# The opening of a fused attention and mixer kernel: batch 1's first transposes one unit earlier, their loads earlier, two dummies, and a new list of PSUM banks

## The chip, the cores and the metric

The kernel runs on one core of one Trainium2 chip. The metric is the device time of one execution in microseconds, and of several executions the median counts. A core has five engines that run side by side and meet at semaphores: TensorE (PE in the profile; its weight loads are PEld), VectorE (DVE), ScalarE (ACT), GpSimd (POOL) and SyncE (SP). TensorE writes to PSUM, which the other engines read and empty. In this kernel POOL's queue issues all loads of q, k, v and of the weights except the very first piece of k, and SP's queue issues the stores and the transposes that are done by DMA.

## The reference

The kernel computes sigmoid attention for 8 batches, 12 heads, 448 positions and a head width of 64, lays the heads side by side as 768 channels, and sends the result through a mixer with a token layer and a channel layer:

```python
S = q.shape[2]
scores = np.matmul(q, k.transpose(0, 1, 3, 2)) / np.sqrt(q.shape[-1]) - np.log(S)
attn = 1.0 / (1.0 + np.exp(-scores))
x = np.matmul(attn, v).transpose(0, 2, 1, 3).reshape(B, S, H * D)

h = np.maximum(x.transpose(0, 2, 1) @ w_tok1, 0.0) @ w_tok2
u = x + h.transpose(0, 2, 1)
out = u + np.maximum(u @ w_ch1, 0.0) @ w_ch2
```

w_tok1 is 448x256, w_tok2 256x448, w_ch1 768x1536 and w_ch2 1536x768. Everything comes in as float32; the loads cast to 16 bits.

## The kernel before

**Units and cycles.** The 12 heads of a batch are worked in three units of four heads, so 8 batches give 24 cycles of one unit each. A unit's 448 positions are seven tiles of 64 (index j). `qk(b, u, j)` makes the scores of one tile: four matmuls of 64x64 into one of two score buffers, and then one sigmoid on ScalarE (line 182) from there into `att`. `av` multiplies `att` by v, tile by tile, into two accumulators (`xa`), and VectorE casts them into `xT` (line 211). `xtrans` turns `xT` into `xn` with 8 transposes on TensorE and one copy on VectorE (lines 235 and 240). `tok1` is the first token layer (8 matmuls, line 280, and a relu), `ytrans` the second (4 matmuls, line 301, and two additions on VectorE, line 308). `ch1` and `ch2` are the channel layers.

**How q and k get their layout.** Scores need q and k with the head width on partitions. For the first units `pe_transpose(b, t, u)` does this on TensorE: 14 transposes of 128x64 (line 155) into one PSUM tile, and one VectorE copy into `tr_q` or `tr_k` (line 164). From batch 2's second unit on it is done by DMA. The transposes of batch 1's unit 0 need only the loads of batch 1's q and k for unit 0, which go into tiles of their own.

**The order of the work is written out by hand.** Each engine takes its instructions in the order in which the program issues them. For batch 0 the list `between` (lines 625 to 653) says what follows each of the seven score tiles of each of the three units; the loop at line 654 issues score tile j and then the entry j. In unit 0 the entries are dummy matmuls (`keep_warm`, line 582, on a tile of zeros into a bank called `heat`, which nobody reads) and transposes for batch 0's later units. In unit 1 they are the values of unit 0, its `xtrans` and its `tok1`, with three empty entries (2, 3 and 5); in unit 2 they are the values of unit 1, the second token layer of unit 0, the transposes of batch 1's unit 0, `xtrans` and `tok1`. Batch 1's unit 0 (lines 662 to 682) is written out too: the rest of batch 0's token layers, the transposes for batch 1's unit 1 and the first pieces of the channel layer. From line 701 on, cycles 4 to 8 take pieces of the channel layers between the scores by shares.

**Loads.** They go out on POOL's queue in the order of lines 500 to 556, each `load` as two DMAs, one for each half of the partitions. At most eight of them are open: where a ninth is due, POOL waits for the oldest.

**Banks.** PSUM has eight banks. The two score buffers take four; everything else takes one of four banks, m0 to m3, through `bank()` (line 79). Up to cycle 8 the digit is read from the string `OPENING_BANKS`, one character for each allocation in the order of issue; after that the banks go round. An accumulator waits until the readers of the one that last stood in its bank are done. So the string decides which earlier readers each accumulator waits for.

Of the kernel before, what the change touches and what calls it, by code (L numbers as in the profile page):

```python
# [20 lines left out]
NJ = 7  # L21
NP = 64
NU = 3
OPENING_BANKS = "0321302130213021213021303021302121302130130210321032103210321021301301201"


@with_exitstack
def kernel(
# [46 lines left out]

    opening_banks = [int(n) for n in OPENING_BANKS]
    at_bank = [0]

    def bank(shape, dtype, name):

        if opening_banks:
            n = opening_banks.pop(0)
        else:
            n = at_bank[0]
            at_bank[0] = (n + 1) % 4
        return pp.tile(shape, dtype, tag=f"m{n}", bufs=1, name=name)
# [7 lines left out]
    def raw_tile(b, t):  # L94
        if (b, t) not in raw:
            tag, bufs = f"raw_{t}", 2 if t == "v" else 1
            if b == 1 and t != "v":
                tag = f"rel_{t}"
            raw[b, t] = pa.tile(
                [128, NU, 2, NJ, E], FP16, tag=tag, bufs=bufs, name=f"raw_{t}_{b}"  # L100
            )
        return raw[b, t]

    def load(b, t, src, u0, u1):

        for g in range(2):
            dst = raw_tile(b, t)[64 * g : 64 * g + 64, u0:u1, :, :, :]
            heads = src[b, 6 * g + 2 * u0 : 6 * g + 2 * u1]
            nc.gpsimd.dma_start(
                out=dst.rearrange("p u hi j e -> p (u hi) (j e)"),  # L110
                in_=heads.rearrange("h (p j) e -> p h (j e)", j=NJ),
            )
# [12 lines left out]
    def tr_tile(b, t):  # L125
        if (b, t) not in tr:
            tr[b, t] = pa.tile(
                [128, NU, NJ, 128], FP16, tag=f"tr_{t}", bufs=2, name=f"tr_{t}_{b}"
            )
        return tr[b, t]  # L130
# [18 lines left out]
    def pe_transpose(b, t, u, j0=0, j1=NJ, on_scalar=False):  # L149
        if j0 == 0:  # L150
            tps[t] = bank([128, NJ, 128], FP16, f"tp_{t}_{b}_{u}")
        ps = tps[t]
        for j in range(j0, j1):
            for hi in range(2):
                nc.tensor.transpose(  # L155
                    out=ps[64 * hi : 64 * hi + 64, j, :],
                    in_=raw[b, t][:, u, hi, j, :],
                    identity=ident[:, :],
                )
        dst, src = tr_tile(b, t)[:, u, j0:j1, :], ps[:, j0:j1, :]  # L160
        if on_scalar:
            nc.scalar.activation(out=dst, in_=src, func=COPYF)
        else:
            nc.vector.tensor_copy(out=dst, in_=src)


    def qk(b, u, j):
        if j == 0:
            att[b, u] = pa.tile(
                [128, 2, NJ, S], FP16, tag="att", bufs=2, name=f"att_{b}_{u}"  # L170
            )
        ps = pp.tile([128, 2, 512], FP32, tag="qk", bufs=2, name=f"qk_{b}_{u}_{j}")
        for g in range(2):
            for hi in range(2):
                nc.tensor.matmul(  # L175
                    out=ps[64 * g : 64 * g + 64, hi, 0:S],
                    lhsT=tr[b, "k"][64 * hi : 64 * hi + 64, u, j, 64 * g : 64 * g + 64],
                    rhs=tr[b, "q"][64 * hi : 64 * hi + 64, u, :, 64 * g : 64 * g + 64],
                    start=True,
                    stop=True,  # L180
                )
        nc.scalar.activation(  # L182
            out=att[b, u][:, :, j, :],
            in_=ps[:, :, 0:S],
            func=SIGMOID,
            bias=bias_t[:, :],
            scale=att_scale,
        )
# [42 lines left out]
    def xtrans(b, u):  # L231
        ps = bank([128, 4, 2, 128], FP16, f"xb_{b}_{u}")
        for g in range(2):
            for t in range(4):
                nc.tensor.transpose(  # L235
                    out=ps[:, t, g, :],
                    in_=xTs[b % 2][:, u, g, 128 * t : 128 * t + 128],
                    identity=ident[:, :],
                )
        nc.vector.tensor_copy(  # L240
            out=xn_tile(b)[:, u, :, :, :].rearrange("s g t d -> s t g d"),
            in_=ps[:, :, :, :],
        )
# [3 lines left out]
    def h1_tile(b, u):  # L247
        if u == 0:
            h1[b] = pa.tile([128, 2, 2, NU, 128], FP16, tag="h1", bufs=2, name=f"h1_{b}")
# [19 lines left out]
    def tok1(b, u, relu_on_vector=False, with_scores=False):  # L269

        if not with_scores:
            h1_tile(b, u)
            one = bank([128, 2, 2, 128], FP32, f"tk_{b}_{u}")
            tks[b] = [one[:, tcb, :, :] for tcb in range(2)]
        ps = tks[b]
        for tcb in range(2):
            cols = slice(128 * tcb, 128 * tcb + 128)
            for t in range(3 if with_scores else 4):
                rows = slice(0, 64 if t == 3 and NU * b + u >= N_FIRST else 128)
                nc.tensor.matmul(  # L280
                    out=ps[tcb],
                    lhsT=w1[rows, t, cols],
                    rhs=xn[b][rows, u, :, t, :],
                    start=(t == 0 and not with_scores),
                    stop=(t == (2 if with_scores else 3)),
                )
        for tcb in range(2):
            dst, src = h1[b][:, tcb, :, u, :], ps[tcb]
            if relu_on_vector:
                nc.vector.tensor_scalar(  # L290
                    out=dst, in0=src, scalar1=0.0, scalar2=None, op0=MAX
                )
            else:
                nc.scalar.activation(out=dst, in_=src, func=RELU)  # L294
# [31 lines left out]
    def ch1(b, cb, d0=0, d1=NDB):  # L326
        if cb == 0 and d0 == 0:
            h2[b] = pa.tile([128, NCB, S], FP16, tag="h2", bufs=1, name=f"h2_{b}")
        if d0 == 0:
            acc[b, cb] = bank([128, 512], FP32, f"c1_{b}_{cb}")  # L330
        ps = acc[b, cb]
        for d in range(d0, d1):
            nc.tensor.matmul(  # L333
                out=ps[:, 0:S],
                lhsT=c1[:, BY_UNIT[d], 128 * cb : 128 * cb + 128],
                rhs=uts[b % 2][:, BY_UNIT[d], 0:S],
                start=(d == 0),
                stop=(d == NDB - 1),
            )
        if d1 == NDB:  # L340
            ch1_out(b, cb, ps)

    def ch1_out(b, cb, ps):
        nc.vector.tensor_scalar(  # L344
            out=h2[b][:, cb, :], in0=ps[:, 0:S], scalar1=0.0, scalar2=None, op0=MAX
        )
# [167 lines left out]
    for par in range(2):  # L514
# [3 lines left out]
            in_=tok_rows[0:6].rearrange("(t par) p c -> par p t c", par=2)[par],  # L518
        )
    nc.gpsimd.dma_start(out=w1[0:64, 3, :], in_=tok_rows[NJ - 1])  # L520
    nc.gpsimd.dma_start(
        out=w2s[:, :, :], in_=moe_w_tok2.rearrange("(tc t) s -> t tc s", tc=2)
    )
    load(0, "v", v, 1, NU)
    load(1, "q", q, 0, 1)
    load(1, "k", k, 0, 1)

    def load_c1(half):
        cols = slice(CC // 2 * half, CC // 2 * half + CC // 2)
        nc.gpsimd.dma_start(  # L530
            out=c1[:, :, cols],
            in_=moe_w_ch1.rearrange("(db d) c -> d db c", db=NDB)[:, :, cols],
        )
# [46 lines left out]
    def keep_warm(n):  # L580
        for _ in range(n):
            nc.tensor.matmul(  # L582
                out=heat[0][:, 0:256],
                lhsT=warm[:, 0:128],
                rhs=warm[:, :],
                start=True,
                stop=True,
            )
# [26 lines left out]
    def tp(b, u, t, j0=0, j1=NJ):  # L615
        return lambda: pe_transpose(b, t, u, j0, j1)

    def value(u, j0, j1):
        return lambda: av(0, u, j0, j1)

    def tok(u):
        return lambda: tok1(0, u, relu_on_vector=True)
# [12 lines left out]
        [  # L635
            [value(0, 0, 3)],
            [value(0, 3, NJ)],
            [],
            [],
            [lambda: xtrans(0, 0), regroup_w2],  # L640
            [],
            [tok(0)],
        ],
        [
            [value(1, 0, 3)],
            [lambda: ytrans(0, 0)],
            [value(1, 3, NJ)],
            [tp(1, 0, "q")],
            [lambda: xtrans(0, 1)],
            [tp(1, 0, "k")],  # L650
            [tok(1)],
        ],
    ]
# [10 lines left out]
    ytrans(0, 1)  # L664
    qk(1, 0, 1)
    av(0, 2, 5, NJ)
    pe_transpose(1, "q", 1)
    qk(1, 0, 2)
    xtrans(0, 2)
    pe_transpose(1, "k", 1)  # L670
    qk(1, 0, 3)
    tok1(0, 2, relu_on_vector=True)
    qk(1, 0, 4)
    for cb in range(2):
        ch1(0, cb, 0, 4)
    ytrans(0, 2)
    qk(1, 0, 5)
    for cb in range(2):
# [205 lines left out]
```

## Time and profile before

| | |
|---|---|
| Executions, us | 364.57, 362.68, 362.68 |
| Median, us | 362.68 |
| The profiled execution, us | 364.3 |
| Its span from first to last instruction, us | 362.5 |
| TensorE busy | 354.4 us, 98% of the span |
| VectorE busy | 185.3 us, 51% |
| ScalarE busy | 169.4 us, 47% |
| POOL busy | 52.9 us, 15% |
| Mean granted TensorE clock | 0.993 of full |

The profile is one execution, taken on the chip. Its page gives the busy time of the engines, the chain of work that ended last, and the costliest groups of instructions. The trace behind it can be asked for rows in order of time. A row of the timeline has the start, the length from the first to the last of its instructions, the engine, the line, the operation, output and input, the number of instructions (x4), and in square brackets how long the engine had stood still before them and what ended that. Rows of one engine can overlap a little, since matmuls are pipelined: the distance from one row's start to the next is the better measure. A row of the view by stretches has the stretch, its length, the busy time of PE, PEld, DVE, ACT and POOL, the granted clock of TensorE, the busy share of the DMA engines, and GB/s. The last number of a row of DMA issues is the time from issue to landing. Times are us from the start of the span.

### The profile page before, as it was taken

The numbers are of one execution on the slowest core, as the hardware profiler recorded it, in microseconds if no ns is written. First come the engines' busy times: TensorE is split into PE (matmuls) and PEld (weight loads), VectorE is DVE, ScalarE is ACT, GpSimd is POOL, SyncE is SP. The second block draws the span as 40 slices with busy tenths as digits, with TensorE's granted clock in tenths as the row PEclk, the third lists the DMA queues.
The fourth block names the chain that finished last, engine by engine and source line by source line (L and its number), as shares of the span: only waits on it lengthen the run. The fifth ranks groups of instructions, "written<-read, shape, count | busy, mean of one in ns | idle before, by whom it ended". The sixth has DMA issues, their size and how long they took to land.

```text
span 362.5 us, 9065 instructions
## 1 busy us (share of the span) xinstructions
PE 354.4 (98%) x4028; PEld 203.4 (56%) x4028; DVE 185.3 (51%) x343; ACT 169.4 (47%) x214; POOL 52.9 (15%) x91
## 2 busy tenths in 40 slices
PE   8899999999999999999999999999999999999995
PEld 5545455555556655666556655666556655555563
DVE  3457557354655555456555555456553345526531
ACT  2987645766338840688018840688018840010000
POOL 8875500110040002100040002100010000000000
PEclk9989999999999999999999999999999999999999
DMA  8999999999899697978979497978964490056014
GB/s 146 173 193 205 204 203 190 143 178 214 160 179 178 82 191 142 199 116 151 219 122 189 100 190 141 195 119 150 212 89 84 92 166 12 0 118 140 14 43 109
DMA packets 103958, 52.09 MB, mean 144 GB/s; under 512 B 76016, under 2 KB 100848, under 8 KB 103920
## 3 DMA queue, kind: packets, MB, share of 16 engines
q1 hardware_dynamic: 78880, 29.70, 44.2%
q0 software_dynamic: 24816, 21.50, 38.4%
q8 instruction: 31, 0.51, 0.5%
q10 hardware_dynamic: 224, 0.33, 0.3%
q14 instruction: 7, 0.06, 0.0%
HBM read 43.45 MB, written 11.01 MB: 150 GB/s over the span
## 4 chain that ended last, share of the span: by engine, by line
PE 94%; ACT 4%; DVE 1%; issue 0%
PE c L333 30%; PE c L356 11%; PE c L375 10%; PE qk L175 9%; PE xa L202 8%; PE tk L280 6%; PE c L434 5%; PE yt L301 5%; PE c L458 5%; ACT att L182 4%; PE heat L582 2%; PE tp_k L155 1%; PE tk L261 1%; PE tp_q L155 1%; DVE ut L308 0%; PE xb L235 0%
## 5 line engine op out<-in xcount | busy, mean ns | idle before, releaser
L182 ACT ACTIVATE att<-qk,att_bias 128x896 f16<-128x896 f32 x168 | 155.3, 1017 | 119.3 <-PE qk L175 119.2
L333 PE MATMUL c<-ut,c 128*128 128x448 f16 x576 | 112.7, 353 | 0.0
L333 PEld LDWEIGHTS <-c 128*128 128x128 f16 x576 | 54.7, 98 | 55.7 <-issue 4.9
L344 DVE TENSOR_SCALAR h<-c 128x448 f16<-128x448 f32 x96 | 59.7, 624 | 45.9 <-PE c L333 45.3
L175 PE MATMUL qk<-tr_q,tr_k 64*64 64x448 f16 x672 | 57.2, 358 | 2.1 <-ACT att L182 2.0
L398 DVE TENSOR_TENSOR o<-un,c 128x384 f32<-128x384 f16 x42 | 23.3, 554 | 49.7 <-PE c L434 30.1
L211 DVE CAST xT<-xa 128x448 f16<-128x448 f32 x48 | 27.7, 618 | 37.4 <-PE xa L202 37.4
L356 PE MATMUL c<-c,h 64*64 64x384 f16 x960 | 46.6, 323 | 0.0
L202 PE MATMUL xa<-att,raw_v 64*64 64x448 f16 x672 | 39.9, 353 | 0.7 <-DVE ut L308 0.7
L375 PE MATMUL c<-c,h 128*128 128x384 f16 x216 | 37.8, 326 | 0.0
L356 PEld LDWEIGHTS <-h 64*64 64x64 f16 x960 | 28.1, 107 | 11.8
L175 PEld LDWEIGHTS <-tr_k 64*64 64x64 f16 x672 | 20.3, 105 | 22.2 <-issue 15.6
L308 DVE TENSOR_TENSOR ut<-xT,yt 128x448 f16<-128x448 f16 x48 | 27.4, 613 | 4.8 <-PE yt L301 4.8
L686 POOL COPY gate<-tr_q 128x2 f16<-128x2 f16 x6 | 1.1, 183 | 193.2 <-DMA tr_q<-rel_q 193.2
L294 ACT ACTIVATE h<-tk 128x256 f16<-128x256 f32 x42 | 14.4, 416 | 31.6 <-PE tk L280 31.6
L375 PEld LDWEIGHTS <-h 128*128 128x128 f16 x216 | 20.4, 98 | 14.5 <-issue 1.8
L202 PEld LDWEIGHTS <-raw_v 64*64 64x64 f16 x672 | 20.4, 108 | 12.2 <-issue 1.9
L280 PE MATMUL tk<-xn,w 128*128 128x256 f16 (+1 forms) x156 | 22.6, 282 | 0.0
L301 PE MATMUL yt<-w,h 128*128 128x448 f16 x96 | 22.0, 353 | 0.0
L434 PE MATMUL c<-c,h 128*128 128x384 f16 x120 | 22.0, 326 | 0.0
L280 PEld LDWEIGHTS <-w 128*128 128x128 f16 (+1 forms) x156 | 13.7, 100 | 7.9 <-issue 5.4
L458 PE MATMUL c<-c,h 128*64 128x384 f16 x192 | 17.3, 328 | 0.0
(53 smaller groups left out, 181.0 us busy)
## 6 DMA issues: line engine op xcount, KB each, us to landing
out_dram<-o SPq DMA_DIRECT2D x48, 192.0 KB, 2.8
c<-in_moe_w_ch_dram POOLq DMA_DIRECT2D x4, 1152.0 KB, 15.2
raw_v<-in_v_dram POOLq DMA_DIRECT2D x12, 336.0 KB, 5.9
raw_k<-in_k_dram POOLq DMA_DIRECT2D x10, 336.0 KB, 7.6
raw_q<-in_q_dram POOLq DMA_DIRECT2D x10, 336.0 KB, 10.3
raw_q<-in_q_dram POOLq DMA_DIRECT2D x14, 112.0 KB, 6.1
out_dram<-o SPq DMA_DIRECT2D x15, 96.0 KB, 2.5
raw_k<-in_k_dram POOLq DMA_DIRECT2D x12, 112.0 KB, 5.6
```

Source lines behind the costliest of these rows:

```text
L175: nc.tensor.matmul(out=ps[64 * g : 64 * g + 64, hi, 0:S], lhsT=tr[b, "k"][64 * hi : 64 * hi + 64, u, j, 64 * g : 64 * g + 64], rhs=tr[b, " ...
L182: nc.scalar.activation(out=att[b, u][:, :, j, :], in_=ps[:, :, 0:S], func=SIGMOID, bias=bias_t[:, :], scale=att_scale,)
L202: nc.tensor.matmul(out=ps[g][64 * hi : 64 * hi + 64, 0:S], lhsT=raw[b, "v"][64 * g : 64 * g + 64, u, hi, j, :], rhs=att[b, u][64 * g : 64 ...
L211: nc.vector.tensor_copy(out=xTs[b % 2][:, u, g, 0:S], in_=ps[g][:, 0:S])
L280: nc.tensor.matmul(out=ps[tcb], lhsT=w1[rows, t, cols], rhs=xn[b][rows, u, :, t, :], start=(t == 0 and not with_scores), stop=(t == (2 if ...
L301: nc.tensor.matmul(out=ps[:, 0:S], lhsT=h1[b][:, tcb, g, u, :], rhs=w2[:, tcb, :, :], start=(tcb == 0), stop=(tcb == 1),)
L333: nc.tensor.matmul(out=ps[:, 0:S], lhsT=c1[:, BY_UNIT[d], 128 * cb : 128 * cb + 128], rhs=uts[b % 2][:, BY_UNIT[d], 0:S], start=(d == 0), ...
L344: nc.vector.tensor_scalar(out=h2[b][:, cb, :], in0=ps[:, 0:S], scalar1=0.0, scalar2=None, op0=MAX)
L356: nc.tensor.matmul(out=ps[p][m : m + 64, 0:n], lhsT=lhsT(p, part, m), rhs=rhs(p, part), start=(first and turn == 0), stop=(last and turn = ...
L375: nc.tensor.matmul(out=ps[:, 0:DH], lhsT=h2[b][:, cb, 128 * t : 128 * t + 128], rhs=c2[:, cb, cols], start=(cb == 0), stop=(cb == NCB - 1 ...
L434: nc.tensor.matmul(out=ps[p][:, 0:DH], lhsT=h2[b][:, n, 128 * t : 128 * t + 128], rhs=c2[:, n, DH * p : DH * p + DH], start=False, stop=(n ...
L458: nc.tensor.matmul(out=ps[g], lhsT=h2[b][:, n, 384:448], rhs=c2[:, n, DH * g : DH * g + DH], start=(n == 0), stop=(n == NCB - 1 and not ad ...
```

## The change

The loads of batch 1's unit 0 move forward: q ahead of v's units 1 and 2 and of w_tok2, k ahead of v's unit 2. The load of v's units 1 and 2 becomes two loads. In `between`, unit 1's empty entries 2, 3 and 5 get two dummies, the transposes of q and those of k for batch 1's unit 0. Unit 2's entry 3 becomes empty, and its entry 5 takes the transposes of q for batch 1's unit 1. Behind it, batch 1's unit 0 is left with the transposes of k for unit 1; the first block of the channel layer moves ahead of the token step. `OPENING_BANKS` is a new string with 74 digits where there were 73 (the second `heat` of unit 1 is the additional allocation). What is computed stays the same.

```diff
-OPENING_BANKS = "0321302130213021213021303021302121302130130210321032103210321021301301201"
+OPENING_BANKS = "23103210320103210323210321210321313021302302132013201320132013213023023123"
...
     nc.gpsimd.dma_start(out=w1[0:64, 3, :], in_=tok_rows[NJ - 1])
+    load(1, "q", q, 0, 1)
+    load(0, "v", v, 1, 2)
     nc.gpsimd.dma_start(
         out=w2s[:, :, :], in_=moe_w_tok2.rearrange("(tc t) s -> t tc s", tc=2)
     )
-    load(0, "v", v, 1, NU)
-    load(1, "q", q, 0, 1)
     load(1, "k", k, 0, 1)
+    load(0, "v", v, 2, NU)
...
         [
             [value(0, 0, 3)],
             [value(0, 3, NJ)],
-            [],
-            [],
+            [new_heat, lambda: keep_warm(2)],
+            [tp(1, 0, "q")],
             [lambda: xtrans(0, 0), regroup_w2],
-            [],
+            [tp(1, 0, "k")],
             [tok(0)],
         ],
         [
             [value(1, 0, 3)],
             [lambda: ytrans(0, 0)],
             [value(1, 3, NJ)],
-            [tp(1, 0, "q")],
+            [],
             [lambda: xtrans(0, 1)],
-            [tp(1, 0, "k")],
+            [tp(1, 1, "q")],
             [tok(1)],
         ],
...
     av(0, 2, 5, NJ)
-    pe_transpose(1, "q", 1)
+    pe_transpose(1, "k", 1)
     qk(1, 0, 2)
     xtrans(0, 2)
-    pe_transpose(1, "k", 1)
     qk(1, 0, 3)
+    ch1(0, 0, 0, 4)
     tok1(0, 2, relu_on_vector=True)
     qk(1, 0, 4)
-    for cb in range(2):
-        ch1(0, cb, 0, 4)
+    ch1(0, 1, 0, 4)
     ytrans(0, 2)
```

## The prediction, made before the changed kernel was run

> **What bounds the kernel now.** I read the page's engine shares first, then the clock in short stretches, then TensorE's timeline in the opening, and at last the places behind it where TensorE stands still.
>
> ```profile
> span 362.5 us, 9065 instructions
> PE 354.4 (98%) x4028; PEld 203.4 (56%) x4028; DVE 185.3 (51%) x343; ACT 169.4 (47%) x214; POOL 52.9 (15%) x91
> ```
>
> TensorE is busy for 98% of the span. A microsecond of its work that moves into a hole, or a hole that closes, therefore reaches the end, unless a transfer then comes too late. The holes lie in the opening. The stretches below give the granted clock (the value behind the five engines), and the timeline gives TensorE's steps: each L175 row is one score, and the distance between two of them is what lies between.
>
> ```profile
> 19.80:19.90 0.10, 0.10 (x4) 0.03 (x3) 0.10 (x1) 0.10 (x1) 0.10 (x1) 0.73 1.26 197
> ...
> 23.20:23.30 0.10, 0.10 (x8) 0.08 (x4) 0.00 (x0) 0.10 (x1) 0.10 (x1) 0.71 1.18 215
> ```
>
> ```profile
> 14.33 0.38 PE L175 MATMUL qk<-tr_q,tr_k 64*64 64x448 f16 x4
> ...
> 15.23 0.38 PE L175 MATMUL qk<-tr_q,tr_k 64*64 64x448 f16 x4
> ...
> 17.02 0.38 PE L175 MATMUL qk<-tr_q,tr_k 64*64 64x448 f16 x4 [0.47 <-ACT att L182]
> 17.92 0.38 PE L175 MATMUL qk<-tr_q,tr_k 64*64 64x448 f16 x4 [0.52 <-ACT att L182]
> 18.24 0.62 PE L235 MATMUL xb<-ident,xT 128*128 128x128 f16 x8
> 18.82 0.38 PE L175 MATMUL qk<-tr_q,tr_k 64*64 64x448 f16 x4
> 19.71 0.51 PE L175 MATMUL qk<-tr_q,tr_k 64*64 64x448 f16 x4 [0.52 <-ACT att L182]
> ...
> 21.98 0.59 PE L175 MATMUL qk<-tr_q,tr_k 64*64 64x448 f16 x4
> ...
> 23.37 0.36 PE L175 MATMUL qk<-tr_q,tr_k 64*64 64x448 f16 x4
> ...
> 24.52 0.38 PE L175 MATMUL qk<-tr_q,tr_k 64*64 64x448 f16 x4
> ...
> 25.49 0.36 PE L175 MATMUL qk<-tr_q,tr_k 64*64 64x448 f16 x4
> ...
> 26.29 0.38 PE L175 MATMUL qk<-tr_q,tr_k 64*64 64x448 f16 x4
> ...
> 27.23 0.38 PE L175 MATMUL qk<-tr_q,tr_k 64*64 64x448 f16 x4
> ...
> 28.06 0.38 PE L175 MATMUL qk<-tr_q,tr_k 64*64 64x448 f16 x4
> ...
> 29.35 0.38 PE L175 MATMUL qk<-tr_q,tr_k 64*64 64x448 f16 x4
> ```
>
> In the second unit (14.33 to 19.71) ScalarE's sigmoids set the pace, and TensorE waits 0.47, 0.52 and 0.52 for them. Then its clock falls to half. Inside the first short stretch 0.73 is 46% at full and the rest at half, so the fall is at 19.85; by the same reading of 0.71 the return is at 23.26. The token step behind the last score shows the price: 19.71 to 21.98 is 2.27, where the third unit's same step, 28.06 to 29.35, takes 1.29.
>
> How this execution stands to the median: it took 364.3, the median is 362.68. I replay the third unit from 19.71 at full clock with the rows' own steps: token step 1.29 gives 21.00; three tiles of values 0.90 (14.33 to 15.23) 21.90; the second token layer 1.15 (23.37 to 24.52) 23.05; four tiles of values 0.97, 24.02; q's transposes 0.80, 24.82; xb 0.94, 25.76; k's transposes 0.83, 26.59; token step 1.29, 27.88. That is 1.47 ahead of the row at 29.35, and 364.3 less 1.47 is 362.8, near the median. So I read the median as an execution without the fall, and 364.3 and 364.57 as executions with it. [...]
>
> **The change part by part.** First the loads. In the list behind the small token weights, q of batch 1 now goes first, then v's second unit, w2s, k of batch 1, v's third unit; cutting v in two adds two issues.
>
> ```profile
> 10.80 0.74 POOL L521 DMA_DIRECT2D w2s<-in_moe_w_tok_dram  x1
> ...
> 12.74 1.25 POOL L109 DMA_DIRECT2D raw_q<-in_q_dram  x2
> ```
>
> ```profile
> L109 POOL DMA_DIRECT2D raw_q<-in_q_dram x2: 654/659/664, 12.7 to 13.3; - x2
> ...
> DMA to landing us min/median/max: 6.5/6.5/6.6
> ```
>
> ```profile
> raw_v<-in_v_dram POOLq DMA_DIRECT2D x2, 112.0 KB, 4.4
> ```
>
> The last row is the pair of first-unit v loads, issued before the queue filled. An issue of 112 KB costs 0.63 (1.25 for two). From 10.80 on: q 10.80 and 11.43, v 12.06 and 12.69, w2s 13.32, k 14.06 and 14.69. When does k's second half land? It is needed behind the sixth score of unit 1, from 18.82 + 0.31 = 19.13. Lower bound: issue plus the short time of the last row, 14.69 + 4.4 = 19.1. Upper bound: issue plus the long time of the row above, 14.69 + 6.6 = 21.3. Between them I go by place in the queue: from 10.80 the old order carries w2s, all of v and q, 224 + 448 + 224 KB by the tiles' shapes, and its last byte lands at 13.33 + 6.5 = 19.85; the new order carries q, v's unit, w2s and k, the same 896 KB. I take 19.85.
>
> Then TensorE. Two dummies stand in the hole ahead of 17.02:
>
> ```profile
> 7.40 0.39 PE L582 MATMUL heat<-warm 128*128 128x256 f16 x2
> ```
>
> 0.39 in a hole of 0.47 costs nothing; without that hole it would be up to 0.39. q's transposes, about 0.51 (the row of the next fence), fit the hole ahead of 17.92, their data having come with 11.43 + 4.4 = 15.8. k's transposes wait for 19.85 and end at 20.36, so unit 1's last score goes at 20.36 instead of 19.71. Queued behind that wait are this score, its sigmoid and the token step. With a full clock, the steps are now: token 1.29, 21.65; values 0.90, 22.55; token layer 1.15, 23.70; values 0.97, 24.67. Here the transposes are gone, and the next limits show:
>
> ```profile
> 8.78 12.68 ACT L182 ACTIVATE att<-qk,att_bias 128x896 f16<-128x896 f32 x14 [0.89 <-PE qk L175]
> ...
> 24.95 4.64 ACT L182 ACTIVATE att<-qk,att_bias 128x896 f16<-128x896 f32 x5 [0.17 <-PE qk L175]
> ```
>
> ```profile
> 25.69 1.16 DVE L211 CAST xT<-xa 128x448 f16<-128x448 f32 x2 [0.30 <-PE xa L202]
> ...
> 34.52 0.61 DVE L164 COPY tr_k<-tp_k 128x896 f16<-128x896 f16 x1
> ```
>
> ```profile
> 33.88 0.51 PE tp_k L155 x14
> ```
>
> A sigmoid follows its score by 0.43 (24.52 to 24.95) and takes 0.91 (12.68 / 14); scores have two buffers, so the score after 24.67 waits for the sigmoid of the one at 23.70, which ends 25.04: it goes at 25.1. The casts start 0.20 behind the score that follows the values (25.49 to 25.69), here 24.87 to 26.03, and the second half of xb, 0.31, waits for them: next score 26.35. That hole was covered by the transposes that left. Then batch 1's second q in place of k, 0.80, 27.15, and the token step, 28.44. Against 29.35 that is 0.91 less, and against the full-clock replay of the old order (27.88) it is 0.56 more.
>
> Batch 1's first unit now has one set of transposes (k) where it had two: 0.51 less. A block of the first channel layer moves ahead of the token step; it is the same work, and it covers the VectorE copy of xn that the removed transposes covered. The extra VectorE copies in unit 1 (0.61 each) lie in a half-idle engine. The channel weights must be there earlier:
>
> ```profile
> 19.61 1.16 POOL L530 DMA_DIRECT2D c<-in_moe_w_ch_dram  x1
> ```
>
> ```profile
> c<-in_moe_w_ch_dram POOLq DMA_DIRECT2D x1, 1152.0 KB, 10.4
> ```
>
> They land at 30.0; the moved block starts near 33. The two extra issues, 1.26 on a queue that mostly waits for earlier transfers, carry no bytes, so I cost them at nothing here and up to 1.3 of lateness as a bound: still covered.
>
> Last, the bank list. Paired with the order of allocations, every accumulator up to batch 2's third unit replaces a predecessor of the same kind as before, under another number. The difference is there: the values of batch 2's second unit took banks from the two token-layer outputs just ahead of them; now they take those of the second channel layer's last outputs.
>
> ```profile
> 54.78 0.57 PE L175 MATMUL qk<-tr_q,tr_k 64*64 64x448 f16 x8
> ...
> 56.51 0.36 PE L175 MATMUL qk<-tr_q,tr_k 64*64 64x448 f16 x4
> ```
>
> ```profile
> 83.62 0.56 DVE L405 COPY o<-c 128x384 f32<-128x384 f32 x1 [2.41 <-PE c L386]
> ...
> 86.48 1.14 DVE L481 COPY o<-c 64x384 f32<-64x384 f32 x2 [1.26 <-PE c L469]
> 87.23 0.57 PE L175 MATMUL qk<-tr_q,tr_k 64*64 64x448 f16 x8
> ...
> 87.66 1.15 DVE L308 TENSOR_TENSOR ut<-xT,yt 128x448 f16<-128x448 f16 x2
> ...
> 88.33 0.38 PE L202 MATMUL xa<-att,raw_v 64*64 64x448 f16 x2 [0.52 <-DVE ut L308]
> ...
> 90.03 0.54 PE L175 MATMUL qk<-tr_q,tr_k 64*64 64x448 f16 x4
> ```
>
> Two scores and the values take 1.73 elsewhere (54.78 to 56.51) and 2.80 here (87.23 to 90.03), because the values wait for the additions of L308. The new predecessors are free at 84.18 and 87.62; TensorE gets there at about 87.63. The gain is 1.07; its bounds are 0 (if I misread the list) and 1.2.
>
> Sum: 364.3 - 0.91 - 0.51 - 1.07 = 361.8, that is 0.9 below the median (0.2%).
>
> **The rivals.** *k is in time.* If it lands by 19.1, unit 1's last score stays at 19.71, and the same steps give 21.00, 21.90, 23.05, 24.02, 24.45 (sigmoid), 25.69 (casts), 26.49, 27.78: 1.57 less than 29.35, 361.15 in all. For it speaks that small loads leave the queue less full; against it the byte count.
>
> [...]
>
> *Slower: k lands at the upper bound.* At 21.2 TensorE has stood for 2.1, the clock falls at 19.85, the transposes take 0.9 until 22.1, and of the token step 0.58 is done by 23.26; it ends 23.97. The rest at full clock is 6.78 (21.00 to 27.78), 30.75: 1.40 behind 29.35. 364.3 + 1.40 - 0.51 - 1.07 = 364.1, slower than the median. At full clock each 0.1 of lateness costs 0.1, so k decides the sign from a landing at about 20.7. Against it: 6.6 was measured behind twice the bytes per issue.
>
> *The bank list brings nothing*, because another wait stands behind the additions: 361.8 + 1.07 = 362.9.
>
> **How the numbers follow.** Forecast (k near 19.85, full clock) 0.45; k in time 0.20; clock still falls 0.20; k at the upper bound 0.08; bank list without effect 0.07. The likeliest is 361.8, its own range 361.4 to 362.3. The range 360.9 to 363.5 takes in all but the k-late case and tails on both sides. Half a per cent, 1.8, is about what a measurement of this kernel can tell from no change; around 362.68 that is 360.9 to 364.5, and nearly all cases lie within. Faster by more than that is k in time with a little more, or a comparison in which most executions of the old kernel carry the fall (two of the four shown do), where 361.8 is 0.7% below 364.3: 0.25. Slower by more is the tail of the late k: 0.07. The rest, 0.68, is within.
>
> **What the new profile would show.** k's transposes in unit 1 start near 19.9, behind a wait of about 0.7 for their load; the granted clock stays at full through 24; the score that stood at 29.35 stands near 28.4; two scores and the values of batch 2's second unit take about 1.75. I am wrong if the clock falls in the new opening, if k lands after 20.7, or if L202 still waits for L308 there.

## The result and the profile after

| | before | changed |
|---|---|---|
| Median of 14 executions each, us | 362.93 | 362.14 |
| Lowest to highest, us | 362.68 to 364.6 | 361.69 to 362.87 |
| Profiled execution, us | 364.3 | 362.46 |
| Its span, us | 362.5 | 360.7 |
| Its mean granted clock | 0.993 | 0.997 |

The ratio goes by the means and is 0.9968, with a 95% interval of 0.9954 to 0.9982: a gain of 0.3%, clear of no change though under the half per cent that I called measurable. By the medians the gain is 0.79. Four of the 14 executions of the kernel before took 364.3 or more, as those with the fall of the clock do; against the median of the other ten, 362.79, the gain is 0.65. Forecast were 361.8 and a range of 360.9 to 363.5.

The page's first lines for the changed kernel:

```profile
span 360.7 us, 9069 instructions
PE 351.7 (98%) x4030; PEld 202.7 (56%) x4030; DVE 185.8 (52%) x343; ACT 169.3 (47%) x214; POOL 53.8 (15%) x93
```

TensorE is the bound as before. Its timeline in the new opening (start, length, line, output and input, and in brackets the standstill ahead of it):

```profile
16.95 0.38 PE L175 MATMUL qk<-tr_q,tr_k 64*64 64x448 f16 x4
17.27 0.58 PE L155 MATMUL tp_q<-ident,raw_q 128*64 128x128 f16 x14
17.85 0.38 PE L175 MATMUL qk<-tr_q,tr_k 64*64 64x448 f16 x4
18.17 0.62 PE L235 MATMUL xb<-ident,xT 128*128 128x128 f16 x8
18.75 0.38 PE L175 MATMUL qk<-tr_q,tr_k 64*64 64x448 f16 x4
20.63 0.58 PE L155 MATMUL tp_k<-ident,raw_k 128*64 128x128 f16 x14 [1.50 <-DMA raw_k<-in_k_dram]
21.14 0.38 PE L175 MATMUL qk<-tr_q,tr_k 64*64 64x448 f16 x4
...
25.33 0.36 PE L175 MATMUL qk<-tr_q,tr_k 64*64 64x448 f16 x4
25.86 0.38 PE L175 MATMUL qk<-tr_q,tr_k 64*64 64x448 f16 x4 [0.16 <-ACT att L182]
26.22 0.93 PE L235 MATMUL xb<-ident,xT 128*128 128x128 f16 x8
...
29.20 0.38 PE L175 MATMUL qk<-tr_q,tr_k 64*64 64x448 f16 x4
```

q's transposes start right behind their score. k's do not: TensorE stands still for 1.50 until the load is there. POOL's loads of k (the instructions that use `raw_k` in that stretch) say when:

```profile
L109 POOL DMA_DIRECT2D raw_k<-in_k_dram x2: 661/662/664, 14.0 to 14.6; - x2
...
DMA to landing us min/median/max: 5.9/5.9/5.9
```

The second half lands at 14.6 + 5.9 = 20.5. The clock holds all the same, at 1.00 from 17.80 to 21.21, the wait for k within it (the columns are the length, PE, PEld, DVE, ACT, POOL, and the clock):

```profile
17.80:21.21 3.41, 1.91 (x36) 1.28 (x34) 2.11 (x3) 2.69 (x3) 3.02 (x5) 1.00 1.19 176
```

The mean of 0.997 comes from the end of this execution: the clock is 0.93 between 351 and 360 and 1.00 up to there.

And the place where the bank list matters, TensorE and VectorE in order of time:

```profile
85.80 1.14 DVE L481 COPY o<-c 64x384 f32<-64x384 f32 x2 [1.25 <-PE c L469]
86.55 0.57 PE L175 MATMUL qk<-tr_q,tr_k 64*64 64x448 f16 x8
...
86.96 1.56 PE L202 MATMUL xa<-att,raw_v 64*64 64x448 f16 x28
86.98 1.15 DVE L308 TENSOR_TENSOR ut<-xT,yt 128x448 f16<-128x448 f16 x2
...
88.28 0.42 PE L175 MATMUL qk<-tr_q,tr_k 64*64 64x448 f16 x4
```

The values run beside the additions of L308 and wait for nothing; two scores and the values take 1.73 (86.55 to 88.28) instead of 2.80.

So the 1.84 between the two profiled executions divide into 0.15 up to the score at 29.20 (29.35 before; 0.07 of it was there already at the score of 16.95, 17.02 before), 0.53 in batch 1's first unit (the two scores at 86.55 stood at 87.23, 0.68 in all by then) and 1.07 at the banks; the 0.09 left is within what two executions differ by.

### The profile page after: what moved, and what is told of

It is laid out like the page before. It is cut to its first block, busy times and chain, and to the rows that moved or that the text cites. A ratio compares the mean times of both kernels' runs of the same rounds, so it can differ in the third digit from the quotient of the medians.

```text
span 360.7 us, 9069 instructions
## 1 busy us (share of the span) xinstructions
PE 351.7 (98%) x4030; PEld 202.7 (56%) x4030; DVE 185.8 (52%) x343; ACT 169.3 (47%) x214; POOL 53.8 (15%) x93
## 4 chain that ended last, share of the span: by engine, by line
PE 92%; POOL 4%; DMA 2%; DVE 1%; issue 1%; ACT 1%; POOLq 0%
PE c L333 31%; PE c L356 11%; PE c L375 10%; PE qk L175 9%; PE xa L202 8%; PE tk L280 5%; PE c L434 5%; PE yt L301 5%; PE c L458 5%; DMA raw_k<-in_k_dram 2%; POOL raw_q L109 1%; POOL raw_k L109 1%; POOL raw_v L109 1%; DVE xT L211 1%; PE tk L261 1%
## 5 line engine op out<-in xcount | busy, mean ns | idle before, releaser
L202 PE MATMUL xa<-att,raw_v 64*64 64x448 f16 x672 | 39.1, 349 | 0.0
L308 DVE TENSOR_TENSOR ut<-xT,yt 128x448 f16<-128x448 f16 x48 | 27.4, 614 | 3.4 <-PE yt L301 3.4
L280 PE MATMUL tk<-xn,w 128*128 128x256 f16 (+1 forms) x156 | 21.8, 274 | 0.0
```

What stands on the lines that cost most here:

```text
L202: nc.tensor.matmul(out=ps[g][64 * hi : 64 * hi + 64, 0:S], lhsT=raw[b, "v"][64 * g : 64 * g + 64, u, hi, j, :], rhs=att[b, u][64 * g : 64 ...
L280: nc.tensor.matmul(out=ps[tcb], lhsT=w1[rows, t, cols], rhs=xn[b][rows, u, :, t, :], start=(t == 0 and not with_scores), stop=(t == (2 if ...
```

## The experiments

The theory after the result: three terms that do not depend on each other. The meeting of banks is worth 1.07. One set of transposes less in batch 1's first unit is worth 0.5. The moved opening costs time, because k is late, and is a gain only against executions in which the clock falls. The rivals: the opening brings the gain and the stall at 87 is made up for later; only dummies, not transposes, hold the clock; not the landing of k but sigmoids or casts bound the opening.

Beside the first four experiments 29 executions of the kernel before have a median of 363.04, beside the last four 22 have one of 362.87. Without the executions with the fall (8 and 3, told by their mean clock) the medians are 362.83 and 362.86.

**The banks alone.**

```diff
 (the kernel before)
-OPENING_BANKS = "0321302130213021213021303021302121302130130210321032103210321021301301201"
+OPENING_BANKS = "2013021302130213130213020213021313021302302132013201320132013213023023123"
```

> The kernel before with its bank string renumbered (0 to 2, 1 to 3, 2 to 1, 3 to 0), so that nothing changes up to cycle 8 but the values of batch 2's second unit take the banks of the second channel layer's last outputs. Theory (three separate terms, the bank meeting is worth 1.07): two scores and the values at about 87 take 1.75 instead of 2.80, L202 no longer waits for L308, and the time is 1.07 below the kernel before, about 361.8 against 362.9. Rival (the gain of the change lies in the opening, and the stall at 87 is made up for later): the stall goes and the time stays at 362.9.

Measured: 361.86 against 363.04, ratio 0.9964 (0.9947 to 0.9981). TensorE at the place, in this kernel's profile:

```profile
87.53 0.57 PE L175 MATMUL qk<-tr_q,tr_k 64*64 64x448 f16 x8
87.93 1.56 PE L202 MATMUL xa<-att,raw_v 64*64 64x448 f16 x28
89.26 0.42 PE L175 MATMUL qk<-tr_q,tr_k 64*64 64x448 f16 x4
```

1.73 from 87.53 to 89.26. The rival falls: nothing gives the microsecond back. Without the fall on either side it is 361.85 against 362.83, 0.98. This part alone is at least as good as the whole change (362.14). The clock's fall is still there: 2 of 12 executions have a mean clock of 0.995 and take 363.1 and 363.4.

**The change without it.**

```diff
 (the changed kernel)
-OPENING_BANKS = "23103210320103210323210321210321313021302302132013201320132013213023023123"
+OPENING_BANKS = "01231023103231023101023102023102121302130130210321032103210321021301301201"
```

> The changed kernel with its bank string renumbered, so that the values of batch 2's second unit again take the banks of the two token-layer outputs ahead of them; the opening is as changed. Theory: 1.07 above the changed kernel, about 363.2, that is 0.2 to 0.3 above the kernel before, since the changed opening alone saves only where the old one has the clock's fall. Rival (the opening brings the gain): it stays at 362.1.

Measured: 363.40, ratio to the kernel before 1.0004 (0.9989 to 1.0019), 1.26 above the changed kernel. TensorE in its profile:

```profile
19.15 0.38 PE L175 MATMUL qk<-tr_q,tr_k 64*64 64x448 f16 x4
21.20 0.58 PE L155 MATMUL tp_k<-ident,raw_k 128*64 128x128 f16 x14 [1.67 <-DMA raw_k<-in_k_dram]
...
87.13 0.57 PE L175 MATMUL qk<-tr_q,tr_k 64*64 64x448 f16 x8
88.23 0.38 PE L202 MATMUL xa<-att,raw_v 64*64 64x448 f16 x2 [0.53 <-DVE ut L308]
88.76 1.51 PE L202 MATMUL xa<-att,raw_v 64*64 64x448 f16 x26 [0.15 <-DVE ut L308]
89.92 0.54 PE L175 MATMUL qk<-tr_q,tr_k 64*64 64x448 f16 x4
```

The stall is back (2.79 from 87.13 to 89.92), and all that the opening does, taken together, brings nothing: it is not faster than the kernel before. Two things cancel in that ratio: none of the 12 executions has the fall, and against the executions of the kernel before without it (362.83) this kernel is 0.57 slower.

**The new order of loads alone.** The kernel before with the changed list of loads (the first hunk of the diff under the loads), nothing else.

> The kernel before with nothing but the new order of loads (q of batch 1 first, v in two pieces, k after w2s). Theory: the old order of work needs these tiles only in the third unit, so the time stays within 0.3 of the kernel before, about 362.9, and k's two loads land near 20.5 as they do in the changed kernel. Rival (the two additional issues or w2s's later landing cost something themselves): 0.5 to 1.3 slower, with POOL or the copy of w2 late.

Measured: 362.92, ratio 0.9996 (0.9982 to 1.0009). Neither the two issues nor the later w2s cost anything that can be measured. k's second half landed at 14.7 + 6.0 = 20.7. One of the 12 executions has the fall (0.993, 364.61). The profile shows an execution of the old order of work without the fall:

```profile
20.02 0.38 PE L175 MATMUL qk<-tr_q,tr_k 64*64 64x448 f16 x4 [0.52 <-ACT att L182]
...
25.96 0.38 PE L175 MATMUL qk<-tr_q,tr_k 64*64 64x448 f16 x4
...
28.07 0.38 PE L175 MATMUL qk<-tr_q,tr_k 64*64 64x448 f16 x4
```

```profile
13.54 14.79 ACT L182 ACTIVATE att<-qk,att_bias 128x896 f16<-128x896 f32 x16
28.57 1.01 ACT L182 ACTIVATE att<-qk,att_bias 128x896 f16<-128x896 f32 x1 [0.24 <-PE qk L175]
```

Unit 1's last score is at 20.02, behind a wait of 0.52 for a sigmoid, and the score that ends the third unit is at 28.07. ScalarE computes 16 sigmoids between 13.54 and 28.33 without a gap, and then waits 0.24 for that score. TensorE has no standstill between 20.02 and 28.07 either. So where the clock holds, ScalarE sets the pace in the second unit, and in the third unit both engines are full and TensorE is the later of the two by only about 0.2.

**k in time.**

```diff
 (the changed kernel)
     load(1, "q", q, 0, 1)
+    load(1, "k", k, 0, 1)
     load(0, "v", v, 1, 2)
     nc.gpsimd.dma_start(
         out=w2s[:, :, :], in_=moe_w_tok2.rearrange("(tc t) s -> t tc s", tc=2)
     )
-    load(1, "k", k, 0, 1)
...
-            [lambda: xtrans(0, 0), regroup_w2],
+            [lambda: xtrans(0, 0)],
             [tp(1, 0, "k")],
-            [tok(0)],
+            [regroup_w2, tok(0)],
```

> The changed kernel with k of batch 1 loaded right behind q, ahead of v's second unit and w2s, and the copy of w2 moved behind unit 1's last score. Theory (the late k costs 1.5 in the opening): k lands near 18.0 (where the v loads land now), its transposes start at 19.1 without a wait, the score at 29.20 comes at about 27.8, and the time is about 1.4 below the changed kernel, 360.7. Rival (sigmoids, casts or the later w2s hold the opening up instead): the wait goes, and the score at 29.20 moves by less than 0.5.

Measured: 361.35, ratio to the kernel before 0.9948 (0.993 to 0.9965), 0.8 below the changed kernel.

```profile
19.43 0.58 PE L155 MATMUL tp_k<-ident,raw_k 128*64 128x128 f16 x14
20.02 0.38 PE L175 MATMUL qk<-tr_q,tr_k 64*64 64x448 f16 x4
...
25.10 0.93 PE L235 MATMUL xb<-ident,xT 128*128 128x128 f16 x8
25.96 0.38 PE L175 MATMUL qk<-tr_q,tr_k 64*64 64x448 f16 x4
...
28.08 0.38 PE L175 MATMUL qk<-tr_q,tr_k 64*64 64x448 f16 x4
```

```profile
9.08 19.25 ACT L182 ACTIVATE att<-qk,att_bias 128x896 f16<-128x896 f32 x21 [0.98 <-PE qk L175]
```

The wait is gone, so the late landing of k was its cause. But the score that ends the third unit stands at 28.08, where the old order of work has it at 28.07 (both with unit 1's last score at 20.02). One set of transposes has left the third unit and another stands in for the second, and the unit is no shorter. What took the place of the set that left are the casts: the score ahead of xb goes 0.27 earlier (24.74 against 25.01), but the second half of xb waits for the casts, xb takes 0.93 instead of 0.70, and the next score stands at 25.96 in both traces. The chain of work that ended last runs through the casts there (24.44 to 25.59). ScalarE, which runs its sigmoids without a gap from 9.08 to 28.33, stands close behind. What is gained is the one set in batch 1's first unit and the banks: 362.9 less 0.5 less 1.07 is 361.3. The expected 360.7 was too low by 0.65. The profiled execution of the changed kernel from which I took the 1.5 is one of its later ones (362.46 against the median of 362.14). It had also reached the wait earlier, with the score that stands at 17.32 here at 16.95, and so stood longer at the load: the score at 29.20 moved by 1.12, not by 1.4.

**Without the two dummies.** `[new_heat, lambda: keep_warm(2)]` of unit 1 becomes `[]`, and their digit leaves the string.

> The changed kernel without the two dummies of unit 1 (and without the bank allocation that they had). Theory (the transposes themselves keep the clock up; the dummies lie in a hole): the time stays within 0.2 of the changed kernel, about 362.1, and no execution shows a mean clock below 0.997. Rival (only the dummies keep it up, transposes do not count): some 3 in 10 executions or more show a mean clock of 0.993 to 0.996 and take 1.2 to 1.5 longer, about 363.5, as the kernel before does in about 3 in 10.

Measured: 362.21, ratio 0.998 (0.9972 to 0.9989), 0.07 from the changed kernel. None of 11 executions has a mean clock below 0.997; beside them 3 of 22 executions of the kernel before have 0.994 and take 364.65 to 364.8. At the three in ten of the rival, none in 11 would come about in 2 of 100 cases. The dummies do nothing here that can be measured. In the profiled execution the wait for k is short:

```profile
19.96 0.58 PE L155 MATMUL tp_k<-ident,raw_k 128*64 128x128 f16 x14 [0.15 <-DMA raw_k<-in_k_dram]
```

It is 0.15, against 1.50 and 1.67 with the same order of loads, for two reasons of about the same size. k landed at 14.6 + 5.3 = 19.9, against 20.5 in the changed kernel's trace, and TensorE got there 0.67 later (the score that stands at 16.95 there is at 17.62 here). Both the landing and the start of the scores differ from execution to execution.

**Transposes in place of all dummies.**

```diff
 (the changed kernel)
-        for _ in range(n):
-            nc.tensor.matmul(
-                out=heat[0][:, 0:256],
-                lhsT=warm[:, 0:128],
-                rhs=warm[:, :],
-                start=True,
-                stop=True,
-            )
+        for m in range(2 * n):
+            nc.tensor.transpose(
+                out=heat[0][:, m % NJ, :], in_=warm[:, 0:128], identity=ident[:, :]
+            )
...
-    keep_warm(23)
+    keep_warm(13)
```

> The changed kernel with every dummy matmul replaced by transposes of the same number of columns (the first 23 by 26 transposes, since the identity is ready only at 3.1), so that nothing but transposes and scores runs on TensorE until the values at 14.3. Theory (transposes count as activity): the clock is at full before 10, 14 transposes take about 0.51 and four scores 0.38 as now, and the time is within 1.0 of the changed kernel. Rival (transposes do not count): with scores alone, some 20% of the time, the clock stays at half until the values begin at 14.3 or later; transposes and scores take nearly twice as long till then, and the time is 1.5 or more above the changed kernel.

Measured: 362.56, ratio 0.9985 (0.9971 to 1.0), 0.4 above the changed kernel. TensorE's first part:

```profile
3.19 2.93 PE L583 MATMUL heat<-ident,warm 128*128 128x128 f16 x26 [3.19 <-POOL ident masks.py:199]
6.80 0.96 PE L155 MATMUL tp_q<-ident,raw_q 128*64 128x128 f16 x14 [0.68 <-DMA raw_q<-in_q_dram]
...
10.23 0.96 PE L175 MATMUL qk<-tr_q,tr_k 64*64 64x448 f16 x8
11.12 1.31 PE L583 MATMUL heat<-ident,warm 128*128 128x128 f16 x12
12.36 0.38 PE L175 MATMUL qk<-tr_q,tr_k 64*64 64x448 f16 x4
...
13.43 0.58 PE L155 MATMUL tp_q<-ident,raw_q 128*64 128x128 f16 x14
```

14 transposes take 0.96 at 6.80 and 0.58 at 13.43, and a score takes 0.38 from 12.36 on, as in the changed kernel. That is later than the 10 that I expected, and well before the values at 16.74, where the rival had long rows up to the values: ahead of 12.36 TensorE has run nothing but transposes and the two scores at 10.23 (0.96, where two take 0.57 at 8.35 in the trace of before). Only the lengths of the rows show this. The column of the granted clock stands at 1.00 from 2.00 to 30.00, so that the shorter rows are a rise of the clock is my reading, and not shown. The rival's 1.5 or more does not show either.

**The new order of work with the old loads.** The changed kernel with the old list of loads.

> The changed kernel with the old order of loads. Theory (the moved transposes are bound by the landings): q's transposes wait from about 17.3 to 19.9 and k's to about 21.1; unit 1's last score comes 0.5 to 1.0 later than in the changed kernel, with a stretch of low activity that makes the clock fall in many executions: 362.9 at full clock, about 364.3 with the fall. Rival (landing times are not what bounds the opening): 362.1.

Measured: 364.70, ratio 1.005 (1.0023 to 1.0076), the only one here that is slower than the kernel before beyond its interval. Four of five executions have a mean clock of 0.990 to 0.993 and take 364.67 to 366.4; the profiled one, at 0.998, takes 363.64.

```profile
17.00 0.38 PE L175 MATMUL qk<-tr_q,tr_k 64*64 64x448 f16 x4
20.15 0.58 PE L155 MATMUL tp_q<-ident,raw_q 128*64 128x128 f16 x14 [2.76 <-DMA raw_q<-in_q_dram]
```

TensorE waits 2.76 for q, and unit 1's last score comes at 22.35, 1.2 later than in the changed kernel (0.5 to 1.0 were expected; a wait for k behind it does not show). In this execution the clock holds (1.00 from 17.10 to 20.50, 0.998 in the mean). That the other four lost it at this hole is likely, but they have no trace, so it is not shown.

**The casts covered too.** The kernel with k in time, and the transposes of q for batch 1's unit 1 at entry 3 of unit 2 in place of entry 5.

> The kernel with k loaded right behind q, and in addition the transposes of q for batch 1's unit 1 at entry 3 of unit 2 instead of entry 5. Theory (with k in time, ScalarE paces the second and third unit without a gap, so covering the casts frees TensorE time that the sigmoids do not let it use): within 0.25 of that kernel, 361.1 to 361.4; the 0.17 wait for the sigmoid ahead of xb goes, and one as long shows up behind it. Rival (the wait for the casts is itself the bound): 0.3 to 0.5 faster, 360.9.

Measured: 361.15, ratio 0.9948 (0.9934 to 0.9961), the lowest median here and 0.2 below the kernel with k in time, by executions that overlap (360.64 to 361.31, and 361.0 to 361.62).

```profile
20.21 0.38 PE L175 MATMUL qk<-tr_q,tr_k 64*64 64x448 f16 x4
...
25.52 0.70 PE L235 MATMUL xb<-ident,xT 128*128 128x128 f16 x8
26.15 0.38 PE L175 MATMUL qk<-tr_q,tr_k 64*64 64x448 f16 x4
26.77 0.38 PE L175 MATMUL qk<-tr_q,tr_k 64*64 64x448 f16 x4 [0.24 <-ACT att L182]
...
28.06 0.38 PE L175 MATMUL qk<-tr_q,tr_k 64*64 64x448 f16 x4
```

xb takes 0.70 instead of 0.93, and the wait for the sigmoid moves behind it (0.24), as expected. From unit 1's last score to the score that ends the third unit it is 7.85 now, against 8.06 with k in time and 8.05 in the old order. So the casts had held about 0.2, less than the rival's 0.3 to 0.5, and then ScalarE sets the pace, by the wait of 0.24 for its sigmoid ahead of 26.77.

## Why the prediction was right

**The median as an execution without the fall: right.** Of the 51 executions of the kernel before that stand beside the experiments, 11 have a mean clock of 0.993 or 0.994 and take 364.27 to 364.8; the other 40 have 0.997 or more and take 362.6 to 363.24. Between the medians of the two groups lie 1.81, where the replay had 1.47. It took 0.90 for the first tiles of values, and the trace of the old order without the fall has 0.78 there (21.31 to 22.09); by that trace's third unit (8.05, against 9.64 from 19.71 to 29.35) the fall costs 1.59. What makes up the rest is not shown. The groups go by the mean clock that the profile gives for each execution; that its loss lies in the opening is seen only in the two traces with the fall, of the kernel before and of the banks alone.

**The landing of k: the right step, but a size too small.** Its place in the queue gave 19.85; it was 20.5, between that and the upper bound of 21.3. The wait was 1.50 instead of 0.7. Bytes ahead in the queue did not settle the landing to better than about 1 us: with the same order of loads k landed between 5.3 and 6.4 after its issue in four traces, and in the trace of the kernel with the banks alone, which has the old order of loads, q and k landed 7.6 after their issue where the trace of before has 6.5:

```profile
DMA to landing us min/median/max: 7.6/7.6/7.6
```

The rival of a landing at the upper bound let the clock fall at 19.85 and come back at 23.26, times carried over, as an estimate, from the trace of before. In the trace of the change without its bank meeting k landed at 14.7 + 6.4 = 21.1, near that bound, and the clock held: it is 0.998 in the mean, and the token layer's 8 matmuls behind the wait take 1.05 (at 22.03), where they take 1.89 (at 20.34) in the trace with the fall of the banks alone. There the late load cost its wait (1.67) and no more.

**The third unit behind it: right.** Sigmoid (0.16 at 25.86) and casts (0.93 for xb) limit it as worked out; from unit 1's last score to the score that ends the unit I had 8.08 (20.36 to 28.44), and it is 8.06 (21.14 to 29.20). With the landing put right the forecast of the profiled execution would have been 362.45, or about 362.6 with the start of the transposes, 20.63; it took 362.46. That this agrees so closely is in part chance, since two executions differ by about 0.1 elsewhere. The median is 0.3 lower.

**What "0.91 saved in the opening" meant** was the weak sentence. It holds against the execution that was profiled, with the fall. Against the other executions the opening costs: the rows say 12.25 from 16.95 to 29.20 in the changed kernel, and 10.75 from 17.32 to 28.07 in the old order without the fall. I had 0.56 for that and it is 1.5 in this execution, or 1.13 by the times of the last scores, since its scores started 0.37 earlier and the load did not. By the medians it is about 0.95: one set of transposes and the banks are worth 1.60, and the change is 0.65 below the executions without the fall. That accounts for the 0.3 by which 361.8 was too low. The part of the opening's cost that comes from the late k was the term set too small. Even with k in time the third unit does not get shorter, since the casts, and 0.2 below them the sigmoids, stand right behind the transposes; the prediction had that (27.78 against 27.88), but left it in the rival.

**One set of transposes, 0.51: right** (0.53). **The banks, 1.07: right**, and alone they are the whole gain (361.86, against 362.14 for the whole change).

**Two dummies at nothing: right**, and they could go. **The clock: right in its outcome.** None of the 14 executions of the changed kernel falls below 0.997, nor does any of the 42 in the five experiments that keep the moved transposes and the new loads (12, 6, 11, 8 and 5). That it might still fall I had given 0.20, an estimate of mine: no run shows what makes it fall. The rival of the experiments by which transposes do not count is not borne out: with transposes in place of all dummies each of the 8 executions has a mean clock of 0.997 or more, and the median is 0.4 above the changed kernel.

When the clock falls stays open. In the trace of before it is 1.00 up to 19.80 and then 0.50 through 23.20; the rows below are the stretch ahead of the fall, about as long as the clock then stays down (19.85 to 23.26), and the first 0.10 at the lower clock:

```profile
16.43:19.85 3.42, 1.92 (x28) 0.93 (x23) 2.08 (x4) 3.42 (x5) 1.97 (x4) 1.00 1.24 192
...
19.90:20.00 0.10, 0.10 (x4) 0.00 (x0) 0.10 (x1) 0.10 (x1) 0.10 (x1) 0.50 1.25 197
```

TensorE is busy for 1.92 of that 3.42. In the old order of work with the new loads alone it is busy for 1.90 of 3.40 at the same place (16.80 to 20.20), with the clock at 1.00 and no fall behind it, and in the stretch of the changed kernel shown above for 1.91 of 3.41, also without a fall. Two other traces have even less and no fall: 1.74 of 3.41 in the change without its bank meeting (17.80 to 21.21, by its rows), and 0.64 of 3.40 in the new order with the old loads (17.10 to 20.50). So the busy time of such a stretch does not tell when the clock falls, and why the changed kernel never showed the fall is not settled.

## What to carry to other kernels

Before work is moved into the holes of an engine, ask whether that engine bounds the stretch that the work leaves, and what stands next behind it: the holes lay where ScalarE set the pace, and in the third unit casts and sigmoids stood right behind the transposes, so that their leaving shortened nothing there. What the move gained (0.53) came from batch 1's first unit. A transfer that is needed earlier should be given more room than its place in the queue suggests, here about 1 us. And a list that assigns buffers deserves a search of its own for accumulators that take the buffer of something just produced: one such meeting cost 1.07, and a renumbering of the list, with no other change, took it away.

## What the runs showed that I had not expected

One and the same program takes about 1.8 more in roughly one of five executions (11 of 51), with nothing but the mean clock to tell them apart (0.993 or 0.994 against 0.997 to 1.000). The landing of the same load, issued at the same place of the same list, differs by about 1 us between executions (5.3, 5.9, 6.0 and 6.4 after its issue in four traces), and one step waits for it. The changed kernel spreads over 361.69 to 362.87, where the old one, apart from the fall, spreads over 362.6 to 363.2 and the kernel with k in time over 361.0 to 361.62; that the wait makes the difference fits, but was not tested by itself. The start of the scores moves too: the score that stands at 16.95 in the changed kernel's trace lies between 17.00 and 17.62 in all other traces but the one with transposes in place of the dummies, so times counted from the start of the span compare to about 0.7 only.
